# First keys loaded as fp32 and cast on the core, narrower token parts in batches 0 and 1, and a new order of instructions in an attention and squared-ReLU kernel

## The chip, the cores and the metric

The kernel runs on one core of a Trainium2 chip. A core has TensorE (PE in the profile: matrix products out of SBUF into PSUM), VectorE (DVE), ScalarE (ACT), GpSimd (POOL) and SyncE (SP). SP, ACT and POOL can issue DMAs; only those of POOL convert fp32 to bf16 on the way here. Each engine takes its instructions in the order in which the program has them and waits on semaphores; between engines nothing else sets the order. The metric is device time in microseconds (us); lower is better.

## The reference

Eight batches, eight heads, 576 tokens, head size 64, 32 packed queries `p` per head. Attention is computed twice: `p` attends to keys and values, and what results is keys and values for `q`. A two-layer net with squared ReLU follows.

```python
def sm_attn(qq, kk, vv):
    s = scale * np.matmul(qq, kk.transpose(0, 1, 3, 2))
    s = s - np.max(s, axis=-1, keepdims=True)
    a = np.exp(s)
    a = a / (np.sum(a, axis=-1, keepdims=True) + 1e-09)
    return np.matmul(a, vv)
p_packed = sm_attn(p, k, v)
out = sm_attn(q, p_packed, p_packed)
...
x = np.ascontiguousarray(attn_out.transpose(0, 2, 1, 3)).reshape(B * S, H * D)
h = x @ w_in
r = np.maximum(h, 0.0)
g = r * r
return (g @ w_out).astype(np.float32)
```

`x` has 4608 tokens of 512, `w_in` is 512 x 2048, `w_out` 2048 x 512. Inputs and output are fp32; the kernel computes its products in bf16.

## The kernel before

All inputs are loaded once, w_in and w_out stay in SBUF. Heads go in two halves (`qd` 0 and 1) of four; a half puts four heads on 128 partitions, 32 rows each. Per batch b the work is, with the names that the planner gives its pieces:

- `Lk, Lv, Lq`: loads of keys, values, queries; `LWI.c.i` and `LWO.c`: loads of w_in in four chunks of 512 columns and of w_out in eight chunks of 256 rows. POOL issues them all (L501, L506, L511, L514), in the order of the string ORDER, which interleaves the weights with batches 0 and 1. `LP`: the packed queries p, in two loads at the very start, batches 0 and 1 by ACT, the others by SP (L487); `P` and `PT` scale and transpose them (L491, L494).
- `Tk` (L521) and `Tq` (L518): VectorE's 32x32 transposes of keys and queries. `S1` (L538): scores of p with the keys; `MX` (L541) their maximum, `EX` (L544) the exponential on ScalarE with its sum, `E` (L550) transposes on TensorE, `EC` the copy out, `PV` (L561) the product with the values, `RC` (L566, L568) one over the sum, `XN` (L571) the packed result, `XQ` and `XM`/`XC` its transposes.
- `M` (L588): packed result times w_in, chunk by chunk, copied to SBUF by `MC`. Since attention's second product and the first layer are both linear, M takes the place of w_in: the first layer is then the second softmax's weights `a2` times M.
- `S2` (L604): scores of the queries with the packed result, in two token parts of 256 and 320; on VectorE `SI` (L608) transposes them, `SM` (L611) takes the maximum, `SU` (L620) subtracts, `SS` (L626, L627) sums and inverts, `SN` (L631) multiplies, `SO` (L637) transposes into a2; `SE` (L623) is the exponential on ScalarE.
- `F1`: the first layer, hidden block fb (128 of 2048) by hidden block, for all 576 tokens in two products of 288 columns (L647), except for batch 0, where the two token parts go one after the other (L674, two blocks at a time: 256 and 320 columns). `R` is the ReLU out of PSUM (L656/L658, L681/L683), `SQ` the square (L664/L666, L689/L691) into gT. Each can run on ScalarE or VectorE.
- `F2` (L697): the second layer, by token tiles of 128 (36 tiles t, 4.5 a batch, 16 blocks each); `FC` copies the result (L462 on ScalarE, L464 on VectorE), `ST` stores it in four DMAs of 64 KB from SP (L712). The last tile goes in two halves of columns (`FZ`, L718).

The order is not written by hand. A planner, class Plan, gets each piece with engine, duration, dependences and the PSUM banks or buffers that it takes, and runs a list schedule at build time with priorities and leanings from a table of constants, TABLE (L217); it emits the instructions in that order, so the order is fixed in the program. PSUM's eight banks are used as three pairs (ps) and two singles (pb). Where the plan leaves a gap on TensorE, it fills it with products of zeros that keep the clock up:

```python
def fills(self, gap, t):
    return max(0, int((gap - 0.15) / (0.2135 if t < self.warm else 0.109))) if gap > 0.35 else 0
...
ORDER = ("k0 v0 q0 a0 a1 a2 a3 b0 b1 k1 b2 b3 v1 b4 b5 q1 b6 b7 "
         + " ".join(f"k{b} v{b} q{b}" for b in range(2, B))).split()
```

At most eight of POOL's loads are under way: the issue of one waits for the landing of the eighth before it. So the time at which POOL issues a load, after a wait, tells when an earlier one landed.

## Time and profile before

| what | value |
|---|---|
| median of 3 runs | 254.4 us (253.84 to 255.28) |
| profiled execution, time | 254.4 us |
| its span | 252.3 us |
| PE busy | 237.9 us (94%), 18.5 of it products of zeros |
| DVE busy | 188.2 us (75%) |
| ACT busy | 145.6 us (58%) |
| POOL busy | 46.4 us (18%) |
| first F1 product (batch 0) | 23.68 us |
| first F1 product of batch 1 | 53.64 us |
| last product ends | 247.4 us |

Busy is the time in which an engine has an instruction under way; products overlap, so the 379 ns that a product of 512 columns takes on average is longer than the 216 ns at which they follow each other in the chain that ended last. A window line gives start and end, length, then for PE, PE's weight loads, DVE, ACT and POOL the busy time and the number of instructions, the granted clock, the DMA engines' share and GB/s. With one line's instructions alone, only the engines that run them are shown. A line of the order in time gives start, length, engine, line, operation, what is written and read, the number of instructions taken together, and in brackets how long the engine stood idle before and what it waited for.

### The profile page before, as it was taken

What the parts mean: (1) busy time and instruction counts of PE and PEld (TensorE: products, weight loads), DVE (VectorE), ACT (ScalarE), POOL (GpSimd) and SP (SyncE); (2) the same over time, 40 slices, a digit from 0 to 9 for tenths busy, and PEclk for the clock granted to TensorE, in tenths of its full rate; (3) what the DMA queues carried; (4) which work ended last, traced back from release to release, by engine and by line L of the source; (5) the groups of instructions that cost most, each with busy time, mean ns of one, the idle gap of its engine ahead of it and who ended that gap; (6) DMA issues with size and microseconds to landing.
All of it is one profiled execution on the core that took longest, in us unless ns stands there. A gap on an engine that the chain in (4) does not pass through costs nothing.

```text
span 252.3 us, 5981 instructions
## 1 busy us (share of the span) xinstructions
PE 237.9 (94%) x2387; PEld 135.8 (54%) x2417; DVE 188.2 (75%) x363; ACT 145.6 (58%) x245; POOL 46.4 (18%) x82
## 2 busy tenths in 40 slices
PE   8999998898999999999999999999999999999992
PEld 6667553355644574356644554674544555575441
DVE  1687898969998999899999999894499922373100
ACT  2226895636554597635944657995523689594011
POOL 8479644323433220000000000000000000000000
PEclk9999999999999999999999999999999999999998
DMA  7999999999999999511112011011124210220332
GB/s 155 204 193 179 207 203 209 207 251 233 204 207 245 219 228 200 108 41 31 42 46 66 21 43 44 3 41 42 44 65 103 53 34 1 59 68 16 88 78 71
DMA packets 26747, 28.70 MB, mean 114 GB/s; under 512 B 5600, under 2 KB 18144, under 8 KB 26720
## 3 DMA queue, kind: packets, MB, share of 16 engines
q0 software_dynamic: 17536, 18.35, 43.7%
q1 hardware_dynamic: 8560, 9.77, 15.0%
q8 instruction: 19, 0.31, 0.5%
q10 hardware_dynamic: 624, 0.20, 0.3%
q14 instruction: 8, 0.07, 0.1%
HBM read 37.22 MB, written 9.44 MB: 185 GB/s over the span
## 4 chain that ended last, share of the span: by engine, by line
PE 51%; DVE 2%; issue 1%; ACT 0%; DVEq 0%
PE pb L697 30%; PE ps L647 16%; PE ps L588 2%; PE pb L718 1%; PE ps L604 1%; PE ps L550 1%; DVE s L608 1%; DVE qT L518 1%; DVE m L611 1%; PE ps L538 1%; PE ps L561 0%; ACT e1T L462 0%; DVE s L620 0%; PE ps L578 0%; ACT o_sb L462 0%
## 5 line engine op out<-in xcount | busy, mean ns | idle before, releaser
L697 PE MATMUL pb<-w_out_b,gT 128*128 128x512 bf16 x498 | 125.3, 379 | 4.0 <-DVE gT L666 1.1
L697 PEld LDWEIGHTS <-gT 128*128 128x128 bf16 x560 | 52.5, 98 | 59.2 <-issue 6.4
L647 PE MATMUL ps<-a,M 128*128 128x288 bf16 x448 | 66.2, 286 | 0.7 <-DVE a L637 0.4
L647 PEld LDWEIGHTS <-M 128*128 128x128 bf16 x448 | 43.5, 98 | 20.2 <-DVE a L637 0.9
L656 ACT ACTIVATE r_b<-ps 128x576 bf16<-128x576 f32 x75 | 44.4, 661 | 10.1 <-PE ps L647 8.3
L666 DVE TENSOR_TENSOR gT<-r_b 128x576 bf16<-128x576 bf16 x77 | 33.2, 450 | 14.4 <-ACT r_b L656 12.7
L462 ACT COPY o_sb<-pb 128x512 f32<-128x512 f32 (+1 forms) x29 | 16.4, 571 | 40.1 <-PE pb L697 28.8
L462 ACT CAST M<-ps 128x1024 bf16<-128x1024 f32 (+1 forms) x27 | 23.5, 904 | 9.9 <-PE ps L588 9.4
L664 ACT ACTIVATE gT<-r_b 128x576 bf16<-128x576 bf16 x35 | 23.5, 683 | 4.2 <-DVE r_b L658 3.9
L658 DVE TENSOR_SCALAR r_b<-ps 128x576 bf16<-128x576 f32 x37 | 25.5, 749 | 0.1
L544 ACT ACTIVATE e<-ps,n 128x576 bf16<-128x576 f32 x16 | 11.8, 738 | 15.3 <-DVE n L541 15.3
L468 PE MATMUL pb<-zero 128*128 128x256 bf16 x137 | 18.5, 290 | 1.1 <-DVE zero L471 1.1
L468 PEld LDWEIGHTS <-zero 128*128 128x128 bf16 x137 | 13.5, 104 | 4.3 <-DVE zero L471 1.1
L623 ACT ACTIVATE e<-s 128x512 bf16<-128x512 f32 (+1 forms) x16 | 10.7, 684 | 8.5 <-DVE s L620 8.3
L541 DVE TENSOR_REDUCE n<-ps 128x1 f32<-128x576 f32 x16 | 11.6, 738 | 4.8 <-PE ps L538 4.7
L518 DVE STREAM_TRANSPOSE qT<-kq_b 128x576 f32<-128x576 f32 x16 | 11.9, 756 | 2.6 <-DMA kq_b<-in_q_dram 2.5
L506 POOL DMA_DIRECT2D v_b<-in_v_dram x16 | 11.2, 709 | 12.1 <-DMA kq_b<-in_k_dram 9.1
L521 DVE STREAM_TRANSPOSE kT<-kq_b 128x576 f32<-128x576 f32 x16 | 11.8, 754 | 1.9 <-DMA kq_b<-in_k_dram 1.9
L464 DVE CAST M<-ps 128x1024 bf16<-128x1024 f32 (+1 forms) x9 | 10.3, 1149 | 4.0 <-PE ps L588 4.0
L626 DVE TENSOR_REDUCE t<-e 128x16 f32<-128x512 bf16 (+1 forms) x16 | 11.7, 729 | 2.0 <-ACT e L623 2.0
L501 POOL DMA_DIRECT2D kq_b<-in_q_dram x16 | 8.9, 558 | 22.1 <-DVE qT L518 10.1
L608 DVE STREAM_TRANSPOSE s<-ps 128x512 f32<-128x512 f32 (+1 forms) x16 | 12.1, 769 | 0.8 <-PE ps L604 0.5
(59 smaller groups left out, 208.6 us busy)
## 6 DMA issues: line engine op xcount, KB each, us to landing
out_dram<-o_sb SPq DMA_DIRECT2D x140, 64.0 KB, 2.0
kq_b<-in_k_dram POOLq DMA_DIRECT2D x16, 288.0 KB, 12.0
kq_b<-in_q_dram POOLq DMA_DIRECT2D x16, 288.0 KB, 12.4
v_b<-in_v_dram POOLq DMA_DIRECT2D x8, 320.0 KB, 11.8
v_b<-in_v_dram POOLq DMA_DIRECT2D x8, 256.0 KB, 11.2
w_in_b<-in_moe_w_in_dram POOLq DMA_DIRECT2D x16, 128.0 KB, 6.1
w_out_b<-in_moe_w_out_dram POOLq DMA_DIRECT2D x8, 256.0 KB, 9.5
p_f<-in_p_dram SPq DMA_DIRECT2D x1, 384.0 KB, 4.4
```

The costliest lines, as they stand in the source:

```text
L462: nc.scalar.copy(dst, src)
L468: nc.tensor.matmul(half(7)[:, :2 * P], lhsT=zero[:, :P], rhs=zero, start=True, stop=True)
L518: nc.vector.transpose(qT[:, qd].rearrange("p s x -> p (s x)").bitcast(F32), kq_of["q", b, qd][:].bitcast(F32))
L521: nc.vector.transpose(kT[:, qd].rearrange("p s x -> p (s x)").bitcast(F32).rearrange("p (x a j2) -> p j2 x a", a=32, j2=2), kq_of["k", b, ...
L544: nc.scalar.activation(e1[:, qd], ps1[b, qd], ACT.Exp, bias=n1[b % 2][:, qd:qd + 1], accum_out=d1[b % 2][:, qd:qd + 1])
L608: nc.vector.transpose(s2[x][:].rearrange("p q j i -> p q (j i)"), ps2[b, x])
L647: nc.tensor.matmul(t[:, c], lhsT=M[b % 2][:, qd, fb * FB:(fb + 1) * FB], rhs=a2[b % 2][:, qd, c * HALF:(c + 1) * HALF], start=(qd == 0), s ...
L656: nc.scalar.activation(dst, src, ACT.Relu)
L658: nc.vector.tensor_scalar_max(dst, src, 0.0)
L664: nc.scalar.activation(dst, r, ACT.Square)
L666: eng.tensor_tensor(out=dst, in0=r, in1=r, op=ALU.mult)
L697: nc.tensor.matmul(po[t], lhsT=gT[:, fb, n0:n0 + P], rhs=w_out_b[:, fb, :], start=(fb == 0), stop=(fb == NFB - 1))
```

## The change

The following is changed; the numbers in the code are parts of the program, not measurements.

- **First keys.** Keys of batch 0, half 0 come as fp32 over SP's queue into the space that gT uses later, and are cast to bf16 by two pieces, 640 columns on VectorE and 512 on ScalarE.
- **p.** Only batch 0's p is loaded at the start; the rest by SP after a one-element memset of its buffer, which VectorE does after the second maximum of batch 0.
- **Queries' second half permuted.** The load of half 1 swaps its two pairs of heads (two DMAs of 64 partitions), so that the packed result keeps the scores' layout in both halves, and RC is one instruction for three.
- **Parts.** Batch 0's tokens go in three parts (128, 192, 256 tokens, with 4, 4 and 2 hidden blocks at a time), batch 1's in two (256, 320), each part with its own S2, softmax and F1. Batch 0's queries are loaded and transposed in two pieces (first 128 tokens, then the rest). F2's tiles wait only for the parts that they touch; the first four tiles may be open at the same time.
- **Loads.** The two DMAs of a w_in piece are planned one by one; batch 1's queries go ahead of w_out's chunk 5.
- **Stores.** Two of the four stores of tile 34 are issued by POOL.
- **Order.** Durations in the planner, the rule for products of zeros and TABLE are new, and with them the order on every engine. In the built program there are 68 products of zeros for 137, 82 loads from POOL for 72, on VectorE 17 ReLUs of 576 columns for 37 and 15 copies of o_sb for 6; ScalarE has 79 for 75 such ReLUs and 23 for 35 squares of 576 columns.

```diff
     def fills(self, gap, t):
-        return max(0, int((gap - 0.15) / (0.2135 if t < self.warm else 0.109))) if gap > 0.35 else 0
+        return max(0, int((0.9 * gap - 0.3) / (0.2135 if t < self.warm else 0.109))) if gap > 0.7 else 0
+ORDER = "k0 v0 x0 a0 y0 a1 a2 a3 b0 b1 k1 b2 b3 v1 b4 q1 b5 b6 b7 k2 v2 q2 k3 v3 q3 k4 v4 q4 k5 v5 q5 k6 v6 q6 k7 v7 q7"
...
-    NKQ, NV, NR, NO = 13, 5, 6, 4
+    NKQ, NV, NR, NO = 13, 5, 5, 4
-    TOKH = (JH[0] * 32, JH[1] * 32)
+    PARTS = {0: ((4, 4), (6, 4), (8, 2)), 1: ((8, 2), (10, 2))}
+
+    def parts(b):
+        return PARTS.get(b, ((8, 0), (10, 0)))
+
+    def span(b, x):
+        o = sum(n for n, _ in parts(b)[:x]) * 32
+        return o, parts(b)[x][0] * 32
...
+        def p_gate():
+            nc.vector.memset(p_f[1][:, :1], 0.0)
...
-        def dma_kq(nm, b, qd, slot):
+        def kq_src(nm, b, qd):
+            return {"k": k, "q": q}[nm][b, qd * QH:(qd + 1) * QH].rearrange("h (a j) d -> (h a) (j d)", j=JT)
+
+        def dma_kq(nm, b, qd, slot, g=None, js=(0, JT)):
             t = kq_of[nm, b, qd] = kq_b[slot]
-            nc.gpsimd.dma_start(t, {"k": k, "q": q}[nm][b, qd * QH:(qd + 1) * QH].rearrange("h (a j) d -> (h a) (j d)", j=JT))
+            w = slice(js[0] * D, js[1] * D)
+            if g is None:
+                nc.gpsimd.dma_start(t[:, w], kq_src(nm, b, qd)[:, w])
+            else:
+                nc.gpsimd.dma_start(t[64 * g:64 * g + 64, w], kq_src(nm, b, qd)[64 - 64 * g:128 - 64 * g, w])
+
+        k0_f = gT[:, 0:2, :].rearrange("p a b -> p (a b)").bitcast(F32)
+        K0 = 10 * D
+
+        def dma_k0(slot):
+            kq_of["k", 0, 0] = kq_b[slot]
+            nc.sync.dma_start(k0_f, kq_src("k", 0, 0))
+
+        def k0_cast(i, eng):
+            w = slice(0, K0) if i == 0 else slice(K0, JT * D)
+            cast(eng, kq_of["k", 0, 0][:, w], k0_f[:, w])
...
-        def tr_q(b, qd):
-            nc.vector.transpose(qT[:, qd].rearrange("p s x -> p (s x)").bitcast(F32), kq_of["q", b, qd][:].bitcast(F32))
+        def tr_q(b, qd, js=(0, JT)):
+            w = slice(js[0] * 32, js[1] * 32)
+            nc.vector.transpose(qT[:, qd].rearrange("p s x -> p (s x)").bitcast(F32)[:, w], kq_of["q", b, qd][:].bitcast(F32)[:, w])
...
         def pp_recip(b):
-            d, r = d1[b % 2], r1[b % 2]
-            nc.vector.reciprocal(r[:, 0:1], d[:, 0:1])
-            for c in (0, 64):
-                nc.vector.reciprocal(r[c:c + 64, 1:2], d[64 - c:128 - c, 1:2])
+            nc.vector.reciprocal(r1[b % 2], d1[b % 2])
...
-        def fh_mm(x, j, u):
-            w, o = TOKH[x], x * TOKH[0]
-            t = ph["h", x, j] = pair(u)[:, :, :w]
-            for e in range(2):
-                fb = 2 * j + e
+        def fh_mm(b, x, j, u):
+            (o, w), e = span(b, x), parts(b)[x][1]
+            t = ph["h", b, x, j] = pair(u)[:, :, :e // 2 * w]
+            for i in range(e):
+                fb, c, m = e * j + i, i // (e // 2), i % (e // 2)
                 for qd in QDS:
-                    nc.tensor.matmul(t[:, e], lhsT=M[0][:, qd, fb * FB:(fb + 1) * FB], rhs=a2[0][:, qd, o:o + w],
+                    nc.tensor.matmul(t[:, c, m * w:(m + 1) * w], lhsT=M[b % 2][:, qd, fb * FB:(fb + 1) * FB], rhs=a2[b % 2][:, qd, o:o + w],
                                      start=(qd == 0), stop=(qd == NQD - 1))
...
+        add("Lk.0.0i", [("SP", 0.45, lambda: dma_k0(0))], level=-300)
+        add("G", [("DVE", 0.06, p_gate)], ["MX.0.1"], level=-99)
+        add("LP.1i", [("SP", 0.5, lambda: p_load(1, 1, B, nc.sync))], ["G"], level=-99)
+        add("KC.0", [("DVE", 0.42, lambda: k0_cast(0, V))], ["Lk.0.0"], level=-10)
+        add("KC.1", [("ACT", 0.48, lambda: k0_cast(1, A))], ["Lk.0.0"], level=-10)
...
-                add(f"ST.{t}", [("SP", 1.8, lambda t=t: store(t))], [f"FC.{t}"], free=[(f"FC.{t}", 0)], lag=2.5, level=L)
+                if t < NT - 2:
+                    add(f"ST.{t}", [("SP", 2.45, lambda t=t: store(t))], [f"FC.{t}"], free=[(f"FC.{t}", 0)], lag=2.0, level=L)
+                    add(f"SD.{t}", [("DMA", 0.5, None)], [f"ST.{t}"], level=L)
+                else:
+                    add(f"ST.{t}.0", [("SP", 1.2, lambda t=t: store(t, parts=(0,)))], [f"FC.{t}"], free=[(f"FC.{t}", 0)], lag=2.0, level=L)
+                    add(f"ST.{t}.1", [("POOL", 1.4, lambda t=t: store(t, parts=(1,), eng=nc.gpsimd))], [f"FC.{t}"], lag=2.0, level=L)
```

On VectorE the new order, where it bears on the starts of batches 0 and 1, is (lines of the changed file): for batch 0 L683 (256 columns), L511 (M), L686, L586 (queries' rest, 448 columns, both halves), L690, L683 (384), L696/L697, L686, L701, L690, L707 (the first part's a2); for batch 1 L586 (half 0), L636, L640, L586 (half 1), L683, L686, L683, L690, L686, L511 (o_sb), L696/L697, L589, L701, L589, L707 (first part), L511 (M), L690, L586 (batch 2, half 0), L754 (ReLU), L511 (o_sb), L586 (batch 2, half 1), L764 (square), L754, L754, L696/L697, L764, L701, two L609 (batch 2's maxima), L511 (o_sb), L707 (second part). F1 of batches 0 and 1 is L744 there, F2 L770, the stores L785.

More of the change, by code (lines that the diff above doesn't have):

```diff
@@ L422, in kernel_impl @@
         v_b = many("v_b", NV, [P, H, (GM + 1) * D], BF16)
-        p_f = many("p_f", 2, [P, 12 * D], F32)
+        p_f = [consts.tile([P, n * D], F32, name=f"p_f{n}") for n in (2, 14)]
         p_b = consts.tile([P, B * NQD, D], BF16, name="p_b")
@@ L774, in f1n @@
-        def f1n(b, fb):
-            return f"SQ.{b}.{fb // 2}" if b in SOLO else f"SQ.{b}.{fb}"
+                    for qd in QDS:
+                        load(f"LWI.{n}.{i}.{qd}", 0.62, lambda n=n, i=i, qd=qd: dma_w_in(n, i, qd), 0.6)
+            else:
+                load(f"LWO.{n}", 1.26, lambda n=n: dma_w_out(n), 0.73)
+        add("G", [("DVE", 0.06, p_gate)], ["MX.0.1"], level=-99)
+        add("LP.1i", [("SP", 0.5, lambda: p_load(1, 1, B, nc.sync))], ["G"], level=-99)
+        add("LP.1", [("DMA", 1.0, None)], ["LP.1i"], lag=2.0, level=-99)
@@ L777, in kernel_impl, with squares @@
+        def squares(b, fb, t0, t1):
+            if b not in PARTS:
+                return [f"SQ.{b}.{fb}"]
+            got = []
+            for x, (_, e) in enumerate(parts(b)):
+                o, w = span(b, x)
+                if o < t1 and t0 < o + w:
+                    got.append(f"Q.{b}.{x}.{fb // e}")
+            return got
+        before = {}
         for b in range(B):
             L = 10.0 * b
+            s2n = [f"S2.{b - 1}.{len(parts(b - 1)) - 1}"] if b else []
             for qd in QDS:
```

240 lines of the change are left out of this document (132 added, 108 removed), and 374 rows, old and new, of the table TABLE.

## The prediction

> **What bounds the kernel now.** I read four views: the forty slices, the windows between the points where TensorE's work changes, the same windows for one line, and the order in time around batch 1 and at the end.
>
> ```profile
> PE   8999998898999999999999999999999999999992
> DMA  7999999999999999511112011011124210220332
> ```
>
> The first row looks as if TensorE were full from the first slice on. It isn't: the second view shows what it does.
>
> ```profile
> L468 PE MATMUL pb<-zero 128*128 128x256 bf16 x137 | 18.5, 290 | 1.1 <-DVE zero L471 1.1
> ```
> ```profile
> 23.60:44.60 21.00, 6.91 (x24) 2.36 (x27) 1.00 1.22 206
> 44.60:53.60 9.00, 8.27 (x37) 3.63 (x38) 1.00 1.21 223
> ```
>
> All 137 products of zeros (they only keep the clock up) fall before 23.6 us; the two windows are of L697 alone, the last product (F2). By 53.6 us 61 of them are recorded, which (a few records are missing) is the 64 that batch 0's four whole token tiles allow. So at 53.6 TensorE has done everything that batch 0 gives, and stands.
>
> ```profile
> 41.98 0.78 DVE L518 STREAM_TRANSPOSE qT<-kq_b 128x576 f32<-128x576 f32 x1 [0.62 <-DMA kq_b<-in_q_dram]
> 42.24 0.55 POOL L501 DMA_DIRECT2D kq_b<-in_q_dram  x1 [0.84 <-DMA kq_b<-in_q_dram]
> 51.71 0.82 DVE L637 STREAM_TRANSPOSE a<-n 128x256 f32<-128x256 f32 x2
> 53.64 2.63 PE L647 MATMUL ps<-a,M 128*128 128x288 bf16 x20
> 55.22 0.78 DVE L518 STREAM_TRANSPOSE qT<-kq_b 128x576 f32<-128x576 f32 x1 [1.19 <-DMA kq_b<-in_q_dram]
> ```
>
> That is the chain which ends last in the first fifth: batch 1's second half of queries lands at about 42, its softmax runs on VectorE until 52.5, and the first F1 product of batch 1 starts at 53.64. The loads are full all this time (9 in slices 2 to 16), so the landing is set by bytes, not by when they are issued. After it:
>
> ```profile
> 65.10:247.40 182.30, 178.24 (x1734) 98.49 (x1756) 137.64 (x265) 110.89 (x184) 10.14 (x17) 1.00 0.40 82
> 247.40:252.30 4.90, 0.00 (x0) 0.00 (x0) 0.00 (x0) 0.37 (x1) 0.00 (x0) 0.79 0.32 80
> ```
>
> TensorE is the bound there (178.2 of 182.3), and 4.9 us of stores close the span. By spacing in the chain (L697 0.216 us, L647 0.123, M 0.032, S1 0.63 a batch) the work of TensorE after 65.1 is 179, so some 3.2 us of it are stalls. The time of the kernel is thus three things: when batch 1's products can start, the stalls behind, and the tail.
>
> **The change, part by part.** The profiled execution took 254.4 us, which is also the median: span 252.3 and 2.1 around it.
>
> Arithmetic on TensorE is the same: F1 of batches 0 and 1 in narrower pieces has the same columns (32x128+32x192+32x256 = 64x288). Would 128 columns cost more than their share? L550 has that width and runs ten in 0.57 us, 0.057 each against 128/512x0.216 = 0.054: 0.1 us in all.
>
> First keys. They go on SP's queue ahead of everything, as fp32 with 576 KB landed instead of 288, and are cast on VectorE (640 columns) and ScalarE (512). No row has this load or an fp32 cast out of SBUF. For the cast the bounds are the bf16 copy of 640 (0.48) and the cast of 512 from PSUM on VectorE scaled to 640 (0.85); I take 0.45 since the source isn't PSUM. For the load: if reading limits, it costs what it does now, 288/205 GB/s = 1.4 us; if writing does, twice that. In between stand the queue totals: the hardware queue wrote 9.77 MB in 15.0% of 252.3 us (258 KB/us), the software queue 18.35 MB in 43.7% (166 KB/us), so 576/258 = 2.2 against 288/166 = 1.7. I take +0.5 for all loads behind it (bounds 0 and +1.4). The early p is 64 KB; the late 448 KB, gated by a memset after batch 0's second maximum, go to about 10 us instead of 1: same bytes, nobody waits for them before 28.
>
> Batch 0. Now keys land at 6.6 and 8.3, scores start at 8.51, S2 at 15.08, and S2, its softmax of 1152 columns and a2 end at 23.42. In the new order the first keys should land near 5.5 (hardware issue at 0.76; p's 4.2 us to landing and half a load more), cast and two transposes of 0.75 put the second maximum's end at 9.9 (now 11.29), S2's first part at 13.2. Then VectorE's queue has the other queries' two transposes (L586, 448 columns) ahead of the first part's subtraction. They wait for loads: up to them are ahead p, k, v, q and one chunk of w_in, 5.1 MB of source at 0.41 MB/us, landing at about 16.3 (the same sum gives 16.3 for the first chunk of w_in now, used at 16.91). Behind them come SU, SS, SN, SO of the first part between the second's, some 2.8 us by rows scaled to 256 and 384 columns: first F1 at 20 instead of 23.7. Its price or gain is nearly nothing at the end: the 3.5 us are filled with F1 work (7.7 us in all) that would have been done before 44.6 anyway, and F2 can't be done before w_out has landed (last chunk 44.9, unchanged). Three further M chunks wait for w_in as now.
>
> Batch 1. One w_out chunk (256 KB, 1.25 us) now comes behind its queries: q1 lands 1.25 earlier, +0.5 for the first keys, +0.2 for halves (the second half of each query load is two DMAs of 144 KB; while the 128 KB loads of w_in ran, at 16 to 23.5, 182 GB/s were moved, against 205 at 40 to 50: 11% of 576 KB is 0.3 at most, 0 at least). So its second transpose starts at 41.5 (bounds 40.7 and 42.5) and ends at 42.3. VectorE's order then is SI .71, SM .65, SI .83, SU .67, SM .80, a copy of o .68, SS .91, two key transposes .76 each (k2 lands by 47.8 and 49.1, both in time), SN .70, SO .44: with 0.7 for S2 in front 51.0, so F1 of the first 256 tokens starts at 51.1, **2.5 earlier**. TensorE is there: from S2 at 43.9 it has 29 F2 and 24 M, 7 us, to 50.9. If it isn't, the start slips by the same amount.
>
> Then the second part. TensorE has 32 products of 256 (3.5), S1 of batch 2 (0.63) and 28 F2 (6.1): work until 61.3. VectorE has a copy of M 1.2, SU .80, then batch 2's queries' transposes, which must wait for their loads: 53.2 and 55.2 now, +0.7. All behind them waits: relus, squares, SS, SN, two maxima, o, SO, 6.8 us by the same rows. 55.9 + .76 + 6.8 = 63.5 at the earliest, where now the same work is done at 65.1+0.4 = 65.5. I take 63.7: **-1.8** (bounds: -3.2 if no load is later and VectorE finds the queries there, +0.5 if the first keys and the halves cost their upper bounds and SO comes 1 us behind them).
>
> VectorE over the whole run. By the built order it has 17 relus of 576 instead of 37 (-15.0), 9 wider ones for batches 0 and 1 instead of 6 (+2.5), 15 copies of o instead of 6 (+6.1), one reciprocal of 0.15 for three (-2.5 in all, queries' half permuted so that both halves have one layout), small ones +3: about 6 us less of 188; ScalarE +5 of 146. It is off the bound after 65, so what it can win are stalls: 0 to 3.2; I take **-0.6**, and 1 us more of them as the other end.
>
> The tail. SP's last issues:
>
> ```profile
> 246.29 1.10 SPq L712 DMA_DIRECT2D out_dram<-o_sb  x2
> 248.76 1.18 SPq L712 DMA_DIRECT2D out_dram<-o_sb  x2
> ```
>
> SP issues four stores of tile 34 (0.59 each) before the last two, though their copy ends at 247.80. With two of the four on POOL they go at 247.83 and end at 249.0, where ScalarE's two end too: -0.9. POOL's two are issued from 246.3; a load from POOL took 4.2 us at best to land, so they may land at 251. I take **-0.8** (0 to -0.9).
>
> Sum: -1.8 - 0.6 - 0.8 = -3.2: 254.4 - 3.2 = **251.2**.
>
> **Rivals.** *Nothing but the tail* (0.12): batch 1 starts earlier, but its second part waits for batch 2's queries until TensorE is where it is now. For it speaks that every wait in the chain above is a load and the total of loads is unchanged; against it that w_out moved. 254.4 - 0.8 = 253.6.
>
> *Loads slow down and VectorE's queue stands behind them* (0.12, slower): there are 82 software loads instead of 72, the first ones of 32 to 64 KB. If the whole stream from 14 to 55.2 ran as w_in did (182 for 205), batch 2's second queries come 4.5 later still, 60.4; with .76+6.8 the second part starts at 68.1, 2.6 behind, less 0.8: 256.2. It decides from 6.5% on (58.6, where 66.3-65.5 eats the tail's gain). Against: landings now follow each other by 1.2 to 1.6 us with eight in flight, so a single load's latency is covered. The Trainium skill, "DMA: Bandwidth & Descriptors", section Bandwidth, tells to make DMAs of at least 1 MiB and has 138 GB/s at 64 KB; the 128 KB loads here at 182 GB/s don't bear that out, as several run at once.
>
> *TensorE cold* (0.06): 68 zero products instead of 137. Now their number a microsecond goes 5, 7, 6 and then 9, 11, 12: the first 3 us run at half rate, though the column of the granted clock says 1.00. If such a stretch comes back in F1 of batch 0, TensorE loses 1.5 us, of which 0.2 to 0.5 are covered before 51: 252.3. The Trainium skill, "TensorE: Matmul & The Clock Gate", Part 1, states that an idle window of about 3.4 us halves the clock; the trace agrees with the half rate at the start (3 us), and the gaps in the new order are at most 2.5 us by my landings.
>
> *More than forecast* (0.15): loads not later, second part at once, and 1.9 of the 3.2 us of stalls go: -3.2 - 1.9 - 0.9 = -6.0: 248.4.
>
> **How the numbers follow.** The forecast itself has 0.55. No change means within 0.5%, 253.1 to 255.7, about what a measurement of this kernel can tell. Faster: 0.55 and 0.06 less a tenth for their upper ends, and 0.15, together 0.70; the tail-only case and that tenth make 0.18; slower 0.12. Range 247.6 to 255.0: from below the fourth rival to just short of the slow one; the forecast's own is 249.5 to 252.9.
>
> **What would show it.** First F1 at 20 us (L744); batch 1's second query transpose (L586) at 41.5 after a wait for its load; first L744 of 256 columns for batch 1 at 51.1 and of 320 at 63.7, with VectorE idle for in_q at 53 to 56 before; last SP issue ending 0.9 after the last copy starts its store, not 2.1. Wrong are the steps if q1 lands later than 42.5, if VectorE doesn't wait for batch 2's queries, or if TensorE reaches 51 with F2 of batch 0 left over. The forecast as a whole fails if idle time of TensorE behind 65 grows by over 2 us.

## The result, and the profile after

The changed kernel took 253.3 us (median of 20, 252.1 to 254.59) beside 254.8 us (20 runs) of the kernel before: ratio 0.9934, interval 0.9915 to 0.9953, so 1.5 us faster where 3.2 had been forecast. The same pair was timed twice more during the experiments: 0.9893 (0.9853 to 0.9933) and 0.9908 (0.9876 to 0.9940). The gain is thus some 1.5 to 2.7 us. The forecast's 1.26% is more than any of the three, though the interval of the second reaches it.

The profiled execution of the changed kernel took 254.59 us, the longest of its 20, with a span of 252.8. The forty slices:

```profile
PE   6567898899799999999999999999999999999991
DMA  6999999999999999840211210110330311230232
```

TensorE's first slices are emptier, and one reason is this group of the costliest instructions:

```profile
L515 PE MATMUL pb<-zero 128*128 128x256 bf16 x68 | 11.1, 325 | 1.1 <-DVE zero L518 1.1
```

Only 68 products of zeros fill the gaps. F2's windows (line L770 alone, columns as before) run from the first F1 product of batch 0, 23.55, to batch 1's S2 and on to its first F1 product, 55.54:

```profile
23.55:46.20 22.65, 8.00 (x29) 2.65 (x33) 1.00 1.20 195
46.20:55.54 9.34, 7.41 (x31) 2.83 (x31) 1.00 1.21 211
```

60 of batch 0's 64 products are recorded by 55.54, 61 before by 53.6 (a few records are missing). But TensorE doesn't stand at that point, in neither kernel. VectorE, then TensorE, ahead of 55.54:

```profile
53.43 0.40 DVE L707 STREAM_TRANSPOSE a<-n 128x256 f32<-128x256 f32 x1
```
```profile
50.78 1.67 PE L770 MATMUL ps<-w_out_b,gT 128*128 128x512 bf16 x7 [0.78 <-DVE o_sb L511]
...
53.68 0.84 PE L653 MATMUL ps<-w_in_b,ppT 64*32 64x512 bf16 x24
54.45 1.25 PE L770 MATMUL pb<-w_out_b,gT 128*128 128x512 bf16 x4
```

The first part's a2 is complete at 53.83, and F1 starts 1.7 us later. TensorE had stood 0.78 us before 50.78, until a copy on VectorE freed a bank of PSUM, and so it still had the products of M and four of F2 ahead of F1. Before the change it was alike: a2 was complete at 52.53 (51.71 + 0.82), and TensorE was at F2 until F1 started at 53.64:

```profile
50.41 3.40 PE L697 MATMUL ps<-w_out_b,gT 128*128 128x512 bf16 x15 [0.67 <-ACT o_sb L462]
```

So the prediction's reading that TensorE stands at 53.6 was wrong.

Batch 1 comes later than before, not earlier. VectorE and TensorE in order of time:

```profile
33.16 0.77 DVE L589 STREAM_TRANSPOSE kT<-kq_b 128x576 f32<-128x576 f32 x1
...
40.59 0.49 DVE L511 COPY e1T<-ps 128x640 bf16<-128x640 bf16 x1 [1.33 <-PE ps L770]
...
44.26 0.24 DVE L640 STREAM_TRANSPOSE pq<-pp 128x64 f32<-128x64 f32 x1
44.78 0.78 DVE L586 STREAM_TRANSPOSE qT<-kq_b 128x576 f32<-128x576 f32 x1 [0.28 <-DMA kq_b<-in_q_dram]
...
66.11 0.69 DVE L511 COPY o_sb<-ps 128x512 f32<-128x512 f32 x1 [1.32 <-DMA out_dram<-o_sb]
```
```profile
55.54 1.94 PE L744 MATMUL ps<-a,M 128*128 128x256 bf16 x16
...
67.28 1.80 PE L744 MATMUL ps<-a,M 128*128 128x320 bf16 x12 [1.21 <-DVE a L707]
```

The keys of batch 1 are transposed from 33.16 on (before 30.03), the second half of its queries at 44.78 (before 41.98). POOL's issue of a later load, which waits for these keys to land, tells when they did; before, then after:

```profile
29.94 0.55 POOL L501 DMA_DIRECT2D kq_b<-in_q_dram  x1 [0.70 <-DMA kq_b<-in_k_dram]
```
```profile
33.20 0.54 POOL L558 DMA_DIRECT2D kq_b<-in_q_dram  x1 [0.43 <-DMA kq_b<-in_k_dram]
```

Over all runs this issue lies at 29.9 to 31.2 in the four profiles with the old order (mean 30.6) and at 31.6 to 33.2 in the fourteen with the changed one (mean 32.4; e14 and e16, with loads in another order, aside): the keys land 1.8 us later on average.

Batch 1's second part starts at 67.28 where the forecast took 65.5 for equal work before. Just ahead of that part VectorE stands 1.32 us: a copy of o_sb waits until a store has landed and its buffer is free. The windows from there to the end of the last copy, and on to the end of the span:

```profile
67.28:248.09 180.81, 177.50 (x1741) 98.82 (x1767) 137.00 (x260) 111.61 (x186) 14.39 (x25) 1.00 0.41 85
248.09:252.80 4.71, 0.00 (x0) 0.00 (x0) 0.00 (x0) 0.01 (x1) 0.00 (x0) 0.83 0.25 68
```

Before, the same two stretches are 182.3 (65.5 to the last copy's end at 247.80) and 4.5. So the sum of this execution against the forecast, with the second profile of the same kernel (run e10 below, span 250.4) beside it:

| term | forecast | this profile | e10's profile |
|---|---|---|---|
| start of batch 1's second part | -1.8 | 67.28 - 65.5 = +1.8 | 65.69 - 65.5 = +0.2 |
| from there to the last copy's end | -0.6 | 180.8 - 182.3 = -1.5 | 180.8 - 182.3 = -1.5 |
| from there to the span's end | -0.8 | 4.7 - 4.5 = +0.2 | 3.9 - 4.5 = -0.6 |
| sum, us | -3.2 | +0.5 (span 252.8 for 252.3) | -1.9 (span 250.4) |

The middle term is the same in both; two executions of one kernel differ in the first 67 us and at the very end. Where the change was meant to win most, it won nothing.

The forecast's 65.5 for equal work before is its own estimate, but the split doesn't hang on it. By the weight loads, of which nearly every one is recorded, both kernels have the same products left from batch 1's first F1 product on. That product starts at 53.64 before and at 55.54 and 53.92 (e10) after, +1.9 and +0.3; from there to the last copy's end it is 194.2 us before and 192.6 in both after, -1.6.

### The profile page after: what moved, and what is told of

It reads as the page before. It is cut to its first block, busy times and chain, and to the rows that moved or that the text cites. A ratio compares the mean times of both kernels' runs of the same rounds, so it can differ in the third digit from the quotient of the medians.

```text
span 252.8 us, 5947 instructions
## 1 busy us (share of the span) xinstructions
PE 231.7 (92%) x2364; PEld 131.0 (52%) x2396; DVE 185.0 (73%) x355; ACT 146.6 (58%) x250; POOL 53.5 (21%) x94
## 4 chain that ended last, share of the span: by engine, by line
PE 65%; DMA 17%; DVE 6%; POOL 4%; ACT 2%; issue 2%; SPq 2%; DVEq 0%; POOLq 0%
PE pb L770 36%; PE ps L717 18%; DMA out_dram<-o_sb 4%; DMA kq_b<-in_q_dram 4%; DMA v_b<-in_v_dram 3%; DMA w_in_b<-in_moe_w_in_dram 3%; DMA kq_b<-in_k_dram 3%; PE ps L744 2%; PE ps L653 2%; SPq L785 2%; PE ps L670 2%; PE pb L791 1%; PE ps L770 1%; POOL w_in_b L578 1%; DVE o_sb L511 1%
## 5 line engine op out<-in xcount | busy, mean ns | idle before, releaser
L770 PE MATMUL pb<-w_out_b,gT 128*128 128x512 bf16 x482 | 119.2, 379 | 2.3 <-issue 1.1
L770 PEld LDWEIGHTS <-gT 128*128 128x128 bf16 x560 | 51.8, 98 | 58.5 <-issue 6.2
L717 PE MATMUL ps<-a,M 128*128 128x288 bf16 x384 | 54.9, 286 | 0.2
L717 PEld LDWEIGHTS <-M 128*128 128x128 bf16 x384 | 37.4, 98 | 13.5
L785 POOL DMA_DIRECT2D out_dram<-o_sb x2 | 1.1, 532 | 148.6 <-ACT o_sb L509 148.6
L693 ACT ACTIVATE e<-s 128x512 bf16<-128x512 f32 (+3 forms) x17 | 11.2, 660 | 16.3 <-DVE s L690 16.3
L744 PE MATMUL ps<-a,M 128*128 128x256 bf16 (+3 forms) x160 | 18.3, 262 | 1.2 <-DVE a L707 1.2
L609 DVE TENSOR_REDUCE n<-ps 128x1 f32<-128x576 f32 x16 | 11.6, 748 | 7.8 <-PE ps L606 7.7
L744 PEld LDWEIGHTS <-M 128*128 128x128 bf16 x160 | 13.7, 98 | 5.8 <-DVE a L707 1.9
L752 ACT ACTIVATE r_b<-ps 128x512 bf16<-128x512 f32 (+2 forms) x23 | 14.1, 650 | 4.3 <-PE ps L744 3.8
L511 DVE COPY o_sb<-pb 128x512 f32<-128x512 f32 x13 | 8.8, 679 | 10.4 <-PE pb L770 7.2
L734 ACT ACTIVATE gT<-r_b 128x576 bf16<-128x576 bf16 x23 | 14.6, 679 | 0.1
L586 DVE STREAM_TRANSPOSE qT<-kq_b 128x576 f32<-128x576 f32 (+2 forms) x18 | 12.3, 689 | 2.7 <-DMA kq_b<-in_q_dram 2.7
L770 PE MATMUL ps<-w_out_b,gT 128*128 128x512 bf16 x46 | 12.2, 379 | 1.6 <-DVE o_sb L511 0.8
L589 DVE STREAM_TRANSPOSE kT<-kq_b 128x576 f32<-128x576 f32 x16 | 12.0, 754 | 2.2 <-DMA kq_b<-in_k_dram 2.2
L683 DVE STREAM_TRANSPOSE s<-ps 128x512 f32<-128x512 f32 (+3 forms) x17 | 12.1, 731 | 1.9 <-PE ps L670 1.7
## 6 DMA issues: line engine op xcount, KB each, us to landing
kq_b<-in_q_dram POOLq DMA_DIRECT2D x7, 288.0 KB, 11.1
```

Source lines behind the costliest of these rows:

```text
L586: nc.vector.transpose(qT[:, qd].rearrange("p s x -> p (s x)").bitcast(F32)[:, w], kq_of["q", b, qd][:].bitcast(F32)[:, w])
L589: nc.vector.transpose(kT[:, qd].rearrange("p s x -> p (s x)").bitcast(F32).rearrange("p (x a j2) -> p j2 x a", a=32, j2=2), kq_of["k", b, ...
L683: nc.vector.transpose(flat(s2, b, x).rearrange("p (q n) -> p q n", q=NQD), ps2[b, x])
L717: nc.tensor.matmul(t[:, c], lhsT=M[b % 2][:, qd, fb * FB:(fb + 1) * FB], rhs=a2[b % 2][:, qd, c * HALF:(c + 1) * HALF], start=(qd == 0), s ...
L734: nc.scalar.activation(dst, r, ACT.Square)
L744: nc.tensor.matmul(t[:, c, m * w:(m + 1) * w], lhsT=M[b % 2][:, qd, fb * FB:(fb + 1) * FB], rhs=a2[b % 2][:, qd, o:o + w], start=(qd == 0) ...
```

## The experiments

All are edits of the changed kernel unless said otherwise. Runs e1 to e4 shared one chip, e5 to e8, e9 to e12, e13 to e16 and the last two others; each ratio is to the kernel before on the same chip, in the same rounds.

**e1: the changed kernel again, as a level.** No edit.

> The changed kernel once more, as the level for the runs beside it. Both theories: ratio to the kernel before near 0.993 (253.3 us). In its profile batch 1's second query transpose should start near 44.8 us, not at the 41.5 of the forecast, and the first F1 product of batch 1's second part near 67, as in the first profile; if it shows 65 or less, that profile was an outlier.

252.83 us, 0.9893 (0.9853 to 0.9933), span 250.4: keys transposed at 31.80, second query transpose at 43.27, second part at 65.68.

**e2: first keys as bf16 by POOL again.**

```diff
-            nc.sync.dma_start(k0_f, kq_src("k", 0, 0))
+            nc.gpsimd.dma_start(kq_b[slot], kq_src("k", 0, 0))
...
-            cast(eng, kq_of["k", 0, 0][:, w], k0_f[:, w])
+            pass
```

> First keys loaded by POOL with the conversion, as before the change; the two casts fall away, all else and the order stay. Theory S (the load stream is late because the fp32 keys write 288 KB more, 1.4 us at 205 GB/s, and because only 117 GB/s were moved from 4 to 6 us, 0.9 us more): batch 1's second queries land 1.4 to 2.3 earlier, transpose at 42.5 to 43.4, time 1 to 2 us less than the changed kernel (251.3 to 252.3). Theory B (the second part of batch 1 is held by an output buffer whose store hasn't landed): at most 0.5 less. Forecast's own step (hardware queue brings the keys sooner and that is worth something): 0.5 more.

252.89 us, 0.9897 (0.9857 to 0.9938); the query transpose is at 45.10, no earlier. The fp32 keys aren't what makes the loads late. Why shows in one window of each kernel (2 to 4 us; the last number is GB/s), this run first, the changed kernel below:

```profile
2.00:4.00 2.00, 2.00 (x11) 1.42 (x10) 0.47 (x1) 0.03 (x1) 2.00 (x4) 1.00 0.76 116
```
```profile
2.00:4.00 2.00, 2.00 (x11) 1.41 (x10) 0.00 (x0) 0.03 (x1) 2.00 (x4) 1.00 0.92 299
```

In the first microseconds POOL's loads haven't come to flow, and what the hardware queues move there is moved in time that is otherwise unused.

**e3: POOL's memsets of v_b moved to VectorE's start.**

```diff
-                nc.gpsimd.memset(v_b[i][:64, :, GM * D:], 0.0)
+                nc.vector.memset(v_b[i][:64, :, GM * D:], 0.0)
```

> The four memsets of the value buffers' padding (1.96 us on POOL at 25.3, between the two key loads of batch 1) are done by VectorE at the start, where it waits for the first load. Theory S: the dip of the loads at 24 to 26 us (132 GB/s instead of 205) goes, 0.7 us of stream: batch 1's queries 0.5 to 1.0 earlier, time 0.4 to 0.9 less. Theory B: no change. Rival: eight loads are under way anyway while POOL is busy, no change in the landing either.

253.39 us, 0.9904 (0.9871 to 0.9938). The dip of the loads at 22 to 26 us stays (156 and 136 GB/s by windows of 2 us): the memsets between the two loads of batch 1's keys don't make it. What does stays open; the kernel before has such a dip too (146 at 20 to 22).

**e4: eight output buffers.**

```diff
-        o_sb = many("o_sb", NO, [P, NE], F32)
+        o_sb = many("o_sb", 8, [P, NE], F32)
...
-                ob[t] = o_sb[u[0] - 14]
+                ob[t] = o_sb[t % 8]
```

> Eight output buffers in turn instead of four taken by the plan; same order. Theory B: VectorE's copies at 57.8 and 66.1 wait no longer for a store to land (0.3 and 1.3 us), second part of batch 1 at 65.7 to 66.0 instead of 67.28, time 0.8 to 1.5 us less (251.8 to 252.5). Theory S: VectorE comes to the copy earlier but the loads hold what follows, at most 0.4 less.

251.71 us beside e1's 252.83, 0.9857 (0.9816 to 0.9898). The copy ahead of the second part doesn't wait any more (VectorE, then TensorE, in order of time):

```profile
64.38 0.68 DVE L511 COPY o_sb<-ps 128x512 f32<-128x512 f32 x1
64.97 0.50 DVE L707 STREAM_TRANSPOSE a<-n 128x320 f32<-128x320 f32 x1
```
```profile
65.56 1.66 PE L744 MATMUL ps<-a,M 128*128 128x320 bf16 x11
```

From first to second part 10.6 us, in e1 11.65 and in the first profile 11.74: the wait for stores costs 1.1 us of the path, and the time falls by 1.1. The intervals of e4 and e1 overlap, but the stretch from batch 1's first F1 product to the last copy's end bears it out: 191.2 us here and 190.9 in e11 and e12, which have eight buffers too, against 192.4 to 194.1 in the eleven profiles of the changed order with four.

**e5: all of p at the start.** p's second load goes right behind the fp32 keys, without the memset that held it back.

```diff
             nc.sync.dma_start(k0_f, kq_src("k", 0, 0))
+            p_load(1, 1, B, nc.sync)
...
-        add("LP.1i", [("SP", 0.5, lambda: p_load(1, 1, B, nc.sync))], ["G"], level=-99)
+        add("LP.1i", [("SP", 0.5, None)], ["G"], level=-99)
```

> The changed kernel, but p's second load (448 KB) goes on SP right behind the fp32 keys, without the memset that holds it back. Theory P (p was moved out of the first microseconds, in which the hardware queues have bandwidth to themselves, into the saturated stretch): the stretch from 4 to 6 us moves some 190 GB/s instead of 117 to 138, batch 1's second query transpose starts at 42 to 43 (43.3 to 45.4 in the four runs so far), batch 1's second part 1 us earlier than 65.7 to 67.3, and the time is 0.8 to 1.5 us below the changed kernel's. Rival N (the bytes are the same wherever they lie): transpose where it was, time within 0.4 us. Rival D (p's 256-byte packets now stand ahead of the second keys): first F1 of batch 0 1 to 2 us later than 23.5, time the same or up to 0.5 us longer.

252.34 us, 0.9882 (0.9859 to 0.9905). The free time is used (4 to 6 us of this run, then of the changed kernel):

```profile
4.00:6.00 2.00, 0.72 (x6) 0.35 (x3) 1.17 (x3) 0.62 (x1) 1.92 (x5) 1.00 1.23 261
```
```profile
4.00:6.00 2.00, 1.09 (x6) 0.45 (x3) 1.35 (x4) 0.62 (x1) 1.93 (x5) 1.00 0.87 117
```

The query transposes at 41.83 and 43.29 have no wait for a load any more; yet the second is no earlier than in e1, and the second part is at 65.76. What holds it now is the work from batch 1's keys on: from the first key transpose to the second query transpose there are 11.1 to 12.6 us in all profiles of the changed order up to e12. The difference from e1's ratio, 0.3 us, is within the intervals.

**e6: both at once**, the loads' start as before the change (edits of e2 and e5).

> First keys as bf16 by POOL without casts and all of p at the start: the loads' start as it was before the change, with everything else of the change kept (w_out's chunk behind the queries, halves, three and two parts, order). Theory P: the load stream is back at before's, less the moved w_out chunk: batch 1's second query transpose at 40.7 to 42, its second part at 64 to 65, time 251 to 252 against some 253. If the transpose still stands at 43 or later, what is late is not the keys and not p but the pieces of the query loads or the order on POOL's queue.

252.86 us, 0.9907 (0.9873 to 0.9940); transpose at 44.46, second part at 67.0. By the expectation's own terms neither the first keys nor p is what makes the loads late.

**e7: zero products by the old rule**, 94 instead of 68, by the old line of `fills`.

> Zero products by the old rule in the gaps (94 instead of 68), same order of everything else. Theory C (the granted clock of 0.50 at 8 to 12 us comes from too few products and costs time at the end): the clock column stays at 0.9 or more up to 24 us, and the time is 0.5 to 1.5 us shorter than the changed kernel's. Rival: the loads set this stretch, so the clock changes in the profile but the time stays within 0.4 us.

0.9934 (0.9905 to 0.9963), not faster. The clock was at 0.50 at 8 to 10 us all the same, so the products that the rule adds didn't keep it up, and this run doesn't tell what a full clock would bring. e10 bears on that.

**e8: the last but one tile's stores all on SP again** (`eng=nc.sync` for `nc.gpsimd`).

> The last but one tile's second half of stores goes back from POOL to SP. As the prediction had it: SP's issue ends 2.1 us behind the last copy instead of 1.1, time 0.8 to 0.9 us longer. Rival: ScalarE's two issues and the landing set the end either way, time within 0.3 us.

253.6 us, 0.9935 (0.9912 to 0.9957). The windows from the last copy's end, here and in e10:

```profile
247.34:251.80 4.46, 0.00 (x0) 0.00 (x0) 0.00 (x0) 0.01 (x1) 0.00 (x0) 0.99 0.29 74
```
```profile
246.50:250.40 3.90, 0.00 (x0) 0.00 (x0) 0.00 (x0) 0.01 (x1) 0.00 (x0) 1.00 0.27 78
```

4.46 is the kernel before's 4.5; in the nine other profiles of runs e1 to e10 it is 3.8 to 4.0. POOL's two stores are worth 0.5 to 0.7 us in the tail; the medians don't resolve it (0.9935 here, 0.9893 and 0.9908 in e1 and e10, with intervals that overlap). The first profile's 4.7 is the exception; ScalarE's two stores landed 3.1 us after their issue there, and 2.1 in e1, e2 and e10.

**e9: batch 0's queries in two loads, not six.**

```diff
+            if b == 0 and nm == "q":
+                if js[0]:
+                    return
+                js = (0, JT)
             w = slice(js[0] * D, js[1] * D)
```

> The changed kernel, but batch 0's queries are loaded by two DMAs of 288 KB, at the place of the first part's loads, instead of six of 64 to 224 KB. Theory L (POOL's loads are limited by their number: about eight are in flight, POOL stands for one to land before it issues the next, and the four more of the change put the stream back by 0.6 us each): POOL issues the last chunk of w_in and batch 1's keys 1.5 to 2.4 us earlier than the run of the changed kernel beside it, batch 1's second query transpose starts at 41.5 to 43, its second part 1 to 2 us earlier, time 1 to 2 us less. Rival B (bytes alone set the landing): the same bytes, transpose at 43.3 to 45 as in the runs so far, time within 0.4 us. Either way batch 0's first part starts later than 23.5, up to 25, since its scores wait for the whole load.

252.22 us, 0.9873 (0.9840 to 0.9907). POOL issues batch 1's first keys at 23.73, in e10 at 23.25, and the transposes come at 32.18 and 43.29. By POOL's later issue the keys landed 0.4 us earlier than in e10 (31.56 for 31.97), not 1.5 to 2.4: the number of loads isn't the main cause either. The median is 1 us below e10's, the spans of the two profiles are the same (250.3 and 250.4); whether there is a gain stays open.

**e10: the changed kernel once more, beside e9, e11 and e12.**

> The changed kernel once more, as the level for the runs beside it: transpose 43 to 45.4, second part 65.7 to 67.3, 180.8 us from there to the end of the last copy, 3.9 from that to the span's end, time 252.3 to 253.6.

253.24 us, 0.9908 (0.9876 to 0.9940). In order of time:

```profile
22.20 1.05 PE L744 MATMUL ps<-a,M 128*128 128x128 bf16 x16
```
```profile
31.71 0.78 DVE L589 STREAM_TRANSPOSE kT<-kq_b 128x576 f32<-128x576 f32 x1 [0.77 <-DMA kq_b<-in_k_dram]
...
43.16 0.78 DVE L586 STREAM_TRANSPOSE qT<-kq_b 128x576 f32<-128x576 f32 x1 [0.18 <-DMA kq_b<-in_q_dram]
```

And a window of the same profile, in which the granted clock (third number from the end) is 0.50, as it is from 10 to 18 us:

```profile
10.00:12.00 2.00, 1.42 (x13) 1.18 (x11) 0.96 (x4) 0.70 (x2) 1.23 (x3) 0.50 1.25 193
```

With the clock down for 8 us this execution has the earliest first F1 product of batch 0 among the profiles of the unaltered changed kernel, 22.20 for 23.55. e5 (0.50 from 8 to 14 us) and e11 (1.00 throughout), which have the same loads as each other, start it at 22.14 and 22.09. No cost of the low clock is to be seen.

**e11: eight buffers and p at the start** (edits of e4 and e5).

> Eight output buffers and p at the start, together. If their gains are separate (1.1 us between batch 1's two parts from the buffers, 0.5 from p): time 251.0 to 251.5, second part at 64.6 or before. If p's place is worth nothing, 251.7 as with the buffers alone.

250.67 us, 0.9817 (0.9777 to 0.9857); second part at 63.78. That is 1.0 us below e4 by the ratios, the buffers alone, but the intervals touch: p's place is worth 0.3 to 1.0 us, if anything.

**e12: these and batch 0's queries whole.**

> Eight output buffers, p at the start and batch 0's queries whole. By theory L the best of all: second part at 63 to 64, time 250 to 251. By rival B as the run without the whole queries, 251 to 251.7.

250.27 us, 0.9792 (0.9751 to 0.9832): 2.1% (1.7 to 2.5) faster than the kernel before and 3.0 us faster than the changed one on the same chip (253.24), the best version found. Its interval overlaps e11's.

**e13: w_out's sixth chunk ahead of batch 1's queries again.** Only the order of four loads; every engine's order is kept.

```diff
+        swap = {'Lq.1.0': 'LWO.5', 'Lq.1.1.0': 'Lq.1.0', 'Lq.1.1.1': 'Lq.1.1.0', 'LWO.5': 'Lq.1.1.1'}
...
-            add(f"{name}i", [("POOL", issue, fn)], list(deps) + old, line="load", level=-200)
+            fns[name] = fn
+            add(f"{name}i", [("POOL", issue, lambda: fns[swap.get(name, name)]())], list(deps) + old, line="load", level=-200)
```

> The changed kernel with w_out's sixth chunk again ahead of batch 1's queries; order of all engines and of all other loads as it was. Theory Q (the queries' landing sets batch 1's scores, as the prediction had it): second query transpose of batch 1 1.25 us later than in the unaltered kernel (44.4 to 45.5 for 43.2 to 44.3), time 1.0 to 1.3 us more, ratio to before 1.00. Theory K (batch 1's keys set it: their softmax must be through before the scores): transpose at most 0.5 later where no load wait stood ahead of it, time 0 to 0.5 us more, ratio 0.990 to 0.994.

255.16 us, 0.9987 (0.9966 to 1.0008): the gain is gone. VectorE in order of time:

```profile
31.80 0.78 DVE L589 STREAM_TRANSPOSE kT<-kq_b 128x576 f32<-128x576 f32 x1 [0.21 <-DMA kq_b<-in_k_dram]
...
43.33 0.78 DVE L586 STREAM_TRANSPOSE qT<-kq_b 128x576 f32<-128x576 f32 x1 [1.90 <-DMA kq_b<-in_q_dram]
...
44.81 0.78 DVE L586 STREAM_TRANSPOSE qT<-kq_b 128x576 f32<-128x576 f32 x1 [0.24 <-DMA kq_b<-in_q_dram]
```

Keys at the same time as in e1, queries 1.5 us later (44.81 for 43.27), second part at 67.34 for 65.68. So the chunk's move is worth what the forecast gave it and slightly more. That it doesn't show as a gain over the kernel before fits the keys and the other loads coming later there: the move brings back about what they lose. This is a reading of the traces; no run puts back the old time of the keys.

**e14: batch 1's keys ahead of w_out's first two chunks.** `a3 k1 b0 b1 b2` in ORDER.

> The changed kernel with batch 1's keys loaded ahead of the first two chunks of w_out instead of behind them (the order of the engines is laid out anew for it, so later instructions move too). Theory K: first key transpose of batch 1 at 29.5 to 31 instead of 31.7 to 33.2, its score transposes begin 1 to 2 us earlier (42 to 43), second part 1 us earlier, time 0.5 to 1 us less. Rival: the products of F2 that then wait for w_out stand ahead in TensorE's queue and take it all back: keys' transpose earlier, but scores where they were, time within 0.4 us or longer.

290.43 us, 1.1378. The planner laid out everything anew and left a hole (window of the whole core):

```profile
107.00:165.00 58.00, 36.26 (x661) 19.87 (x660) 49.46 (x94) 31.23 (x57) 3.56 (x6) 0.62 0.22 36
```

TensorE works 36 of 58 us there. Of what the run was for, the first 45 us say this much: keys transposed at 30.78, a microsecond earlier, but TensorE stands 1.37 us for w_out ahead of F2 at 32.88, the keys' scores come behind that, and the queries' transpose is at 43.91. As the rival had it, the place where TensorE waits moves; the time as a whole says nothing on it. The second part's start, 62.54, comes behind another order of products and shows no gain.

**e15: the kernel before with eight output buffers** (e4's edit there).

> The kernel before with eight output buffers instead of four. If the wait for stores to land is the change's own (VectorE copies 15 of the outputs instead of 6): time within 0.4 us of before. Rival: the buffers hold up the kernel before as well: 0.5 to 1.2 us less.

253.12 us, 0.9917 (0.9894 to 0.9939): this one edit of the old kernel brings as much as the whole change. The first expectation had been nothing. The windows behind 67 us, this run first, then before:

```profile
67.00:247.40 180.40, 179.71 (x1758) 98.48 (x1756) 137.11 (x265) 110.67 (x184) 10.16 (x17) 1.00 0.40 82
```
```profile
67.00:247.40 180.40, 176.34 (x1719) 97.41 (x1742) 135.83 (x261) 109.64 (x182) 9.61 (x16) 1.00 0.39 81
```

By these windows TensorE's idle time falls from 4.1 to 0.7 us, but part of that is missing records: from 68 to 240 us the old profile has 429 records of F2 products for 454 weight loads, this run 455 for 455. A missing record leaves a gap of some 0.05 us (two products at 216 ns each, less the 379 ns of one), so about 1.3 us of the fall is an estimate of what was never idle. The stretch from batch 1's first F1 product to the last copy's end doesn't hang on records: 194.2 us before, 193.0 here, 1.2 us less with no work taken off any engine. The rest of the 2.1 us by the ratio isn't in this profile, the longest (254.1) of the run's six executions.

What ScalarE had waited for is a row of the old profile's list of waits (total, times, longest), beside the changed kernel's:

```profile
ACT o_sb L462 <- DMA out_dram<-o_sb: 6.2, 4, 2.3
```
```profile
DVE o_sb L511 <- DMA out_dram<-o_sb: 1.6, 2, 1.3
```

ScalarE stood four times with a copy whose buffer's store hadn't landed, ahead of the copies at 79.9, 84.1, 102.2 and 188.5 us, with ReLUs and exponentials queued behind.

**e16: e11 with the keys first.**

> Eight output buffers, p at the start and batch 1's keys ahead of w_out. By theory K 249.5 to 250.3, ratio 0.977 to 0.980 (0.9817 without the keys' move). By its rival 250.5 to 251.5.

287.03 us, 1.1231: the hole of e14, and no more to be read.

**e17: the kernel before with only the moved chunk** (e13's way, reversed).

> The kernel before with one edit: w_out's sixth chunk is loaded behind batch 1's queries instead of ahead of them. The queries' second transpose stood 0.62 us for its load there, and the keys' softmax was through at 40.5, so the transpose comes up to 0.6 us earlier (first half's transpose at 40.6 is then held by VectorE's own work) and so does everything behind: time 0.4 to 0.8 us less. Rival (the forecast's term as it stood): the whole 1.25 us. Rival: nothing, since batch 2's queries or the stores hold the rest.

256.3 us, 1.0047 (1.0024 to 1.0070): slower, which none of the three expectations had. The queries' transposes come without a wait, at 41.6, and TensorE stands instead:

```profile
42.92 0.81 PE L697 MATMUL pb<-w_out_b,gT 128*128 128x512 bf16 x3 [2.10 <-DMA w_out_b<-in_moe_w_out_dram]
```

F2 products that need the chunk stand ahead of batch 1's S2 in TensorE's queue; S2 starts at 45.69 instead of 42.41, and batch 1's first F1 product at 56.40 instead of 53.64. ScalarE's four waits for stores are still there (5.4 us).

**e18: the kernel before with chunk, eight buffers and the tail's stores.** The tail's edit was given to tile 34, which in that order is not the last but one to be copied (POOL issued at 239.89), so it did nothing.

> The kernel before with the moved chunk, eight output buffers and the last but one tile's second half of stores from POOL. If the three add up: 2.0 + 0.6 + 0.5 = 3.1 us less, ratio 0.988, as good as the whole change or better. If the buffers' and the chunk's gains overlap: 2.5 us, 0.990.

254.97 us, 0.9996 (0.9974 to 1.0019): the buffers' gain and the chunk's loss cancel. Batch 1's first F1 product comes 2.85 us later than before (56.49), and from there to the last copy's end it takes 2.7 us less. Against e17, with the same late start, that stretch falls from 192.7 to 191.4, again 1.2 us, and ScalarE's waits for stores are gone. In these runs the moved chunk pays only with the new order around it.

## Where the forecast failed

The kernel did become faster, but that the sign was right is in part luck: the term that was to bring most brought nothing, and the gain came from the middle term, for another reason than the one given. All three terms were off.

*Batch 1 (-1.8 forecast, +1.8 and +0.2 measured)* is the step that failed, and first in the sentence "So its second transpose starts at 41.5 (bounds 40.7 and 42.5)". The chunk's 1.25 us in it were right (e13: 1.5 at the transposes, 0.5% to 0.9% of the time). What was mis-sized is the cost of later loads beside it: +0.7, at most 1.7, and all of it on the queries. In the fourteen profiles of the changed kernel and its edits up to e13, the transpose lies at 42.7 to 45.4. Two things are in it.

First, the keys, which the forecast followed only for batch 2, land later: 1.8 us on average, 3.3 us between the two first profiles (33.20 for 29.94). Some 0.6 us of the latter is luck of the old profile, the earliest of the four with the old order. The fp32 keys, the memsets, p's place and the number of query loads were each excluded as the main cause (e2, e3, e5, e9), and the first keys and p together (e6). No run put all of them back at once, so why the keys land later stays open.

Second, from those keys to the query transpose it takes 11.1 us or more. The keys' softmax runs over VectorE, ScalarE and TensorE, with ReLUs and squares of batch 0 in between on VectorE, and in the first profile VectorE waits 1.33 us for TensorE in it. So even with the queries there (e5), 43 is about as early as it gets with keys at 31.7. Before, VectorE was through with the keys' work at 41.36, 11.3 us after 30.03, and stood 0.62 us for the queries: no more than that was to be had by moving their load alone.

From that transpose to the first part it is 10.8 us in the first profile and in e10, not 9.6. VectorE's share was forecast well: 9.05 us to the end of a2 (44.78 to 53.83), where 9.5 had been counted. The rest failed in the sentence "TensorE is there": it came to F1 1.7 us after a2, as the result section shows, with F2 of batch 0 left over, which the prediction had named as a sign of being wrong. Before, the same way took 11.7 us (41.98 to 53.64), so it became 0.9 us shorter where the forecast had counted on 2.1.

From first to second part it is 11.7 us, not 12.6. But VectorE wasn't held there by batch 2's queries, as the step had it: in the first profile they had landed (56.05, no wait), and a wait for them shows in three of the fourteen profiles only, 1.33 us at most. It was held by an output buffer, 1.1 us in e4 and up to 1.4 by e11 and e12 (10.3 us).

*Stalls behind (-0.6 forecast, -1.5 measured).* The size was under the mark, and the reason was not borne out. VectorE's busy time fell by 3.2 us (188.2 to 185.0), not by "about 6", and ScalarE's rose by 1.0, not 5. What the runs do show is stores: in the kernel before ScalarE waited 6.2 us for them to land, and eight buffers alone take 1.2 us out of this stretch with no work taken off any engine (e15, and e18 against e17). In the changed order those waits on ScalarE are gone; of the two smaller ones on VectorE that have come, the list's longest lies ahead of 67.28. What else is in the 1.5 us no run splits. The list of waits of the old profile had the row; the forecast read only that TensorE's stalls were 3.2 and looked for their cause in an engine's load.

*Tail (-0.8 forecast, +0.2 and -0.6 measured).* Right in mechanism: 4.5 became 3.8 to 4.0 in nine profiles, and it is back at 4.46 with the stores on SP (e8).

*First keys.* The casts began at 4.62, earlier than the 5.5 of the forecast, and the fp32 bytes cost nothing (e2). But the second half's keys, POOL's first load, set the second maximum: it ended at 11.17, forecast 9.9, and first F1 came at 23.55, not 20. Two rows of VectorE in the first profile show the order of the two:

```profile
4.62 0.49 DVE L511 CAST kq_b<-gT 128x640 bf16<-128x640 f32 x1 [3.35 <-DMA gT<-in_k_dram]
...
8.38 0.78 DVE L589 STREAM_TRANSPOSE kT<-kq_b 128x576 f32<-128x576 f32 x1 [2.20 <-DMA kq_b<-in_k_dram]
```

That this is worth nothing at the end, as forecast, is not shown. First F1 at 22.20 (e10) and 23.86 (e9) goes with spans of 250.4 and 250.3, but 23.55 (first profile) and 24.50 (e3) with 252.8 and 252.7; the same loads set both, and no run separates them.

*The rivals.* "Only the tail" had the time nearest (253.6), but for another sum: three terms that partly cancel, not one. "Loads slow down" was half there: the loads came later by about what the moved chunk gave, and the time still fell, because the stretch behind gave 1.5. "TensorE cold" came true in the clock, and no cost of it is seen in the time (e10).

## What to carry to other kernels

Look through the whole list of waits for a store that frees a buffer, however small, before putting an engine's stalls down to its load; doubling the buffers is a small edit that tests it. Before reading idle time of TensorE as stalls, compare the records of its products with those of its weight loads: missing ones made 3.4 us of a gain that was 1.2 to 2.1. Before moving a load forward, find what else must be done at the same point, and what in the other engines' queues needs the load that it is moved past: here the keys' chain ended 0.6 us ahead of the queries, and in the old order the moved chunk alone made TensorE wait (e17). Profile a kernel twice when the first fifth hangs on loads: the same program differed by 1.6 us there.

## What was not expected of the hardware

- The granted clock fell to 0.50 at 10 to 12 us of the first profile after two gaps of TensorE of 1.14 and 2.29 us between 5 and 9.2, where it had worked 0.69 and 0.79 of two 2-us windows. The Trainium skill, "TensorE: Matmul & The Clock Gate", Part 1, has it fall after an idle window of about 3.4 us; here no gap was that long. In e6 TensorE worked 0.28 us of the window from 6 to 8 us and the clock stayed at 1.00, so these runs give no rule for when it falls.
- A store of 64 KB took 5.2 us (median) from issue to landing between 40 and 100 us, while loads ran, in both kernels, and 2.0 from 100 us on. It fits the places of ScalarE's four waits for a free buffer in the kernel before: three lie before 103 us.
- In the first microseconds 261 (e5) and 299 GB/s (first profile) were moved in a window of 2 us, by the hardware queues together with POOL's first loads; without the keys on SP's queue it was 116 (e2), and from 24 to 46 us of the first profile it was 195.
